# Delta rule into a maxout FFN: evictions of the opening by half of the heads, and the second chunk's first link moved behind x of the first

## The chip, the cores and the metric

The kernel runs on one core of a Trainium2 chip. The metric is the device time of one execution in microseconds, from its start to its end on that core. Before the change it was measured in six runs: the median is 542.86 us, the runs lie between 540.11 and 547.58 us. One of them was recorded by the hardware profiler; its trace is what the profile below shows. "The span" is the time from the first to the last instruction in that trace.

## What is computed

Two layers follow each other. The first is a delta-rule attention: for each of 4 x 8 heads, a state matrix of 48 x 48 is carried over 768 tokens. The second is a feed-forward layer whose hidden value is the largest of three products.

```python
# q, k, v: (B, H, S, D) = (4, 8, 768, 48); beta: (4, 8, 768)
k_n = k / (norm(k) + 1e-6)
for t in range(S):
    y[:, :, t] = q[:, :, t] @ state
    v_old = k_n[:, :, t] @ state
    state = state + beta[t] * outer(k_n[:, :, t], v[:, :, t] - v_old)
x = y.transpose(0, 2, 1, 3).reshape(B * S, H * D)        # 3072 x 384
h = max(x @ w1, x @ w2, x @ w3)                           # 3072 x 768
out = h @ w_out                                           # 3072 x 384
```

The arithmetic is in float32. The weights come as 64-bit floats; the kernel reads their bits and converts them to float32 itself.

## The kernel before, in words

**Chunks.** The 768 tokens are cut into 12 chunks of 64 (`C = 64`), and the recurrence is carried from chunk to chunk. Two batches lie on the 128 partitions (rows `0:64` and `64:128`, called `bb`), and two more in a free dimension (`g`). All eight heads of all four batches are worked on together. Two chunks make a group of 512 tokens, the unit of the feed-forward layer, so there are six groups `m`. Inside a chunk the dependence of the tokens on each other is a triangular system. It is solved in blocks:

- `solve(m)` (line 518) inverts the diagonal blocks for the two chunks of a group on VectorE (DVE), one column at a time: lines 562 and 566, a product and a subtraction. Ahead of that it works out the norms of the keys (`norm`, lines 256 to 265, L258 on ScalarE (ACT), L259 to L263 on DVE), and writes the diagonal (L539, on ACT for every group but the first; it waits for `bl` of L538). For groups 0 and 1 the blocks are 16 wide, for the later ones 32. For group 0 its last part transposes the result (L570) and copies it into `ut[0]` and `ut[1]`, the inverse of each chunk (L581 on ACT; L583 on DVE for chunk 0, on GpSimd (POOL) for chunk 1). For group 1 the result goes to DRAM (L588) and is read back into `ut` (L597) by DMAs that the SyncE queue (SP) issues.
- For chunks 0 to 3 the 16-wide blocks are joined into 32-wide ones: `halves_t` transposes `ut` (L643, L645), `halves_z` (p_e, L671; eviction to `z`, L674) and `halves_u` (p_f, L688; negation into `ut`, L678 on DVE and L680 on ACT).
- For every chunk the 32-wide blocks are joined: `turn_t1` (L629, L631), `join_z` (p_z, L705; evictions L708 and L710), `join_u` (p_j, L719; negation again).
- Then `old_k` and `old_q` multiply the keys and queries with the state (p_k, p_q, L736), `new` makes the new values u (p_u, L764, eviction L769), `to_y` the outputs (p_y, L806; L810 for chunk 0, L808 for the others), `to_x` transposes them into `xt`, the input of the feed-forward layer (p_x, L820, eviction L872/L873 for chunk 0, L870 otherwise), and `step` adds to the state (p_s, L787, L794).

`new` also zeroes a corner of `ut` for the first two chunks (L774, on ACT), which must be zero when the chunk after next is written there.

**PSUM.** All of these links take their PSUM tile from one pool of three buffers (`ps_two`, line 81), in turn. The feed-forward layer has two buffers of its own. `heads_of` (line 647) gives, for chunk 0, two halves of the heads with a PSUM tile each and a copy engine each (ACT for the first, DVE for the second); for other chunks one tile with all heads and ACT. In before, only some evictions use the engine that `heads_of` names; `negated`, `join_z` and `copied` split one PSUM tile between ACT and DVE by partitions.

**The feed-forward layer.** `ffn(m)` (line 911) is a generator: it yields after each group of three accumulating matmuls p_h (L922) with its eviction (L930 a copy on ACT for the first weight, L936 a maximum with `h` on DVE for the others), and later after each p_o (L954). For group 0 the first three slices of hidden units are worked on in two halves of 256 tokens, so that the first half of the tokens (chunk 0) can be used before chunk 1 is ready.

**The weights.** `weights()` (line 219) converts one piece of 128 x 384 at each call of `some(conv, 1)`: ACT makes `mant` and `up` (L232, L233) of a piece, and DVE (L243, L247) and POOL (L251) join the piece before it. A piece's staging buffer (`w_bits`, five of them) is filled by `fetch` on SP (L213).

**The order.** The order of the instructions on each engine is that of the program text; there is no scheduler, and each engine takes its instructions in that order. The opening is written out by hand (lines 990 to 1070); after it the loop over `ffn(0)` (line 1127) runs, in iteration i, the links that the table `FIRST[i]` names ("e1" is halves_z(1), "f1" halves_u(1), "s0" step(0), "T2" the transposes of queries 2, "S1" one step of the current solve), then those of `EARLY_LINKS[i]`, and a conversion. Groups 1 to 5 follow in a loop of their own.

Of the kernel before, what the change touches and what calls it, by code (L numbers as in the profile page):

```python
# [16 lines left out]
BL = 32  # L17
# [4 lines left out]
def kernel(  # L22
# [31 lines left out]
    nc = tc.nc  # L54
# [5 lines left out]
    KT = DM // 128  # L60
# [5 lines left out]
    NK, NQ, NU = 8, 3, 2  # L66
# [451 lines left out]
    def solve(m):  # L518
# [49 lines left out]
        if m == 0:  # L568
            back = in_rows(xs[0])
            nc.vector.transpose(out=back, in_=y.rearrange("p c i -> p i c"))  # L570
            yield
            for cc in range(2):
                for i in range(4):
                    bb, half = divmod(i, 2)
                    r = block(bb, half)
                    to = ut[cc][r, :, :, BL * half : BL * (half + 1)].rearrange(
                        "p g h i -> p (g h) i"
                    )
                    of = back[r, :, 16 * cc : 16 * (cc + 1)].rearrange("p i x -> p x i")
                    if half:  # L580
                        nc.scalar.copy(to, of)  # L581
                    else:
                        (nc.gpsimd if cc else nc.vector).tensor_copy(to, of)  # L583
                yield
            return
        y_d = dram.tile([2, 2, B, H, BL, BL], FP32, name="y_d")
# [72 lines left out]
    def span(hs):  # L659
        return slice(hs[0], hs[-1] + 1)  # L660

    def halves_z(c):
        if c > 1:
            halves_t(c)
        at = [ats[2 * c + g] for g in range(2)]
        second = ut[c % NU].rearrange("p g h (f two x) -> p g h f two x", two=2, x=HB)
        for hs, p_v, copy in heads_of(c, "p_e", BL):
            for i, h in enumerate(hs):
                for bb, g in TILES:
                    r = rows(bb)  # L670
                    nc.tensor.matmul(  # L671
                        p_v[rows(bb ^ g), g, i], at[g][r, h], second[r, g, h, :, 1]
                    )
            copy(zs[c % NU][:, :, span(hs)], p_v)  # L674

    def negated(bb, to, of, c=0):
        if bb and c < 2:
            nc.vector.tensor_scalar_mul(to, of, -1.0)  # L678
        else:
            nc.scalar.mul(to, of, -1.0)  # L680

    def halves_u(c):
        t, z = fine.pop(c), zs[c % NU]
        for hs, p_v, _ in heads_of(c, "p_f", BL):
            for i, h in enumerate(hs):
                for bb, g in TILES:
                    r = rows(bb ^ g)
                    nc.tensor.matmul(p_v[rows(bb), g, i], t[g][r, h], z[r, g, h])  # L688
            for f in (0, 1):
                for bb in range(2):  # L690
                    r = block(bb, f, HB)
                    negated(
                        bb,
                        ut[c % NU][r, :, span(hs), BL * f + HB : BL * (f + 1)],
                        p_v[r, :, :, HB * f : HB * (f + 1)],
                    )

    def join_z(c):
        at = [ats.pop(2 * c + g) for g in range(2)]
        z, second = zs[c % NU], ut[c % NU][:, :, :, BL:C]  # L700
        for hs, p_v, _ in heads_of(c, "p_z", BL):
            for i, h in enumerate(hs):
                for bb, g in TILES:
                    r = block(bb, 1)
                    nc.tensor.matmul(  # L705
                        p_v[block(bb ^ g), g, i], at[g][r, h, 0:BL], second[r, g, h]
                    )
            nc.scalar.copy(z[block(0), :, span(hs)], p_v[block(0)])  # L708
            copy = nc.vector.tensor_copy if c < 2 else nc.scalar.copy
            copy(z[block(1), :, span(hs)], p_v[block(1)])  # L710

    def join_u(c):
        z, t = zs[c % NU], t1[c % NU]
        u12 = ut[c % NU][:, :, :, BL:C]
        for hs, p_v, _ in heads_of(c, "p_j", BL):
            for i, h in enumerate(hs):
                for bb, g in TILES:
                    r = block(bb ^ g)
                    nc.tensor.matmul(p_v[block(bb), g, i], t[r, g, h], z[r, g, h])  # L719
            for bb in range(2):  # L720
                negated(bb, u12[block(bb), :, span(hs)], p_v[block(bb)], c)


    xts, rhss, qss, us, yts = {}, {}, {}, {}, {}
# [33 lines left out]
    def new(c):  # L758
        rhs = rhss.pop(c)
        u = us[c] = both("u", D, 2)  # L760
        for hs, p_v, copy in heads_of(c, "p_u", D):
            for i, h in enumerate(hs):
                for bb, g in TILES:
                    nc.tensor.matmul(  # L764
                        p_v[rows(bb ^ g), g, i],
                        ut[c % NU][rows(bb), g, h],
                        rhs[rows(bb), g, h],
                    )
            copy(u[:, :, span(hs)], p_v)  # L769
        if c + NU < 2 * FINE:  # L770
            for bb in range(2):
                corner = ut[c % NU][block(bb), :, :, BL:C]
                zero = kpad[0][block(bb), None, 0:1, D : D + 1]
                nc.scalar.copy(corner, zero.to_broadcast(corner.shape))  # L774
# [37 lines left out]
    def to_x(c):  # L812
        m, cc = divmod(c, 2)
        if m not in xts:
            xts[m] = work.tile([128, KT, TOK], FP32, name="xt")
        y_f = yts.pop(c).rearrange("p g h d -> p g (h d)")
        p_x = ps_two("p_x")
        for g in range(2):
            for t in range(KT):
                nc.tensor.transpose(  # L820
                    p_x[:, g, t * 128 : (t + 1) * 128],
                    y_f[:, g, t::KT],
                    ident,
                )
        xt = xts[m][:, :, cc * 256 : (cc + 1) * 256].rearrange(
            "p t (g x) -> p g t x", g=2
        )
        copied(c, xt, p_x[:, :, 0 : KT * 128].rearrange("p g (t x) -> p g t x", t=KT))

    yds, yqs = {}, {}  # L830

# [24 lines left out]
    def turn_y(c):  # L856
# [6 lines left out]
            ),  # L863
            in_=yqs.pop(c).rearrange("p b (x t) -> p b t x", t=KT),
        )

    def copied(c, to, of):

        if c:
            nc.scalar.copy(to, of)  # L870
        else:
            nc.scalar.copy(to[:, 0], of[:, 0])  # L872
            nc.vector.tensor_copy(to[:, 1], of[:, 1])  # L873


    def less_first(f):
        part = (slice(None), slice(None), slice(f * 128, (f + 1) * 128))
# [166 lines left out]
    for c in range(2):  # L1044
        scale(c, nrm_0[:, c])
    some(conv, 1)
    halves_u(0)
    turn_t1(0)
    join_z(0)
    masked(pts[0], by_par(pts[0]))  # L1050
    join_u(0)
    masked(pts[1], by_par(pts[1]))
    old_k(0)
    old_q(0)
    some(solving, 1)
# [12 lines left out]
    load_v(2)  # L1068
# [58 lines left out]
    for i, _ in enumerate(ffn(0)):  # L1127
# [83 lines left out]
```

## Time and profile before

| what | value |
|---|---|
| median of six runs | 542.86 us (540.11 to 547.58) |
| the profiled execution | 547.58 us, span 545.9 us |
| TensorE (PE) busy | 507.5 us, 93% of the span |
| DVE busy | 316.0 us, 58% |
| ACT busy | 155.2 us, 28% |
| POOL busy | 167.0 us, 31% |
| mean TensorE clock that was granted | 0.946 of full |
| in the first 110 us: PE, DVE, ACT, POOL busy; clock | 83.0, 83.4, 52.3, 35.0 us; 0.77 |
| from 160 to 487 us: PE, DVE, ACT, POOL busy; clock | 324.0, 191.0, 70.7, 116.6 us; 0.99 |

Times in the trace count from the first instruction of the span. A line of the chain of waits has a start, a duration, an engine and a line of the kernel; "issue" is time in which the engine waited for nothing that the trace shows. A line of a timeline has a start, a duration, the engine, the line, the operation, output and inputs by their names, shapes, the count, and in brackets how long the engine was idle before and what ended that. A float32 matmul of the program is recorded as two, so 32 matmuls appear as x64. SPq is SP's queue of DMA issues.

### The profile page before, as it was taken

The numbers are of one execution on the slowest core, as the hardware profiler recorded it, in microseconds if no ns is written. First come the engines' busy times: TensorE is split into PE (matmuls) and PEld (weight loads), VectorE is DVE, ScalarE is ACT, GpSimd is POOL, SyncE is SP. The second block draws the span as 40 slices with busy tenths as digits, with TensorE's granted clock in tenths as the row PEclk, the third lists the DMA queues.
The fourth block names the chain that finished last, engine by engine and source line by source line (L and its number), as shares of the span: only waits on it lengthen the run. The fifth ranks groups of instructions, "written<-read, shape, count | busy, mean of one in ns | idle before, by whom it ended". The sixth has DMA issues, their size and how long they took to land.

```text
span 545.9 us, 18537 instructions
## 1 busy us (share of the span) xinstructions
PE 507.5 (93%) x8096; PEld 315.1 (58%) x8096; DVE 316.0 (58%) x701; ACT 155.2 (28%) x285; POOL 167.0 (31%) x279
## 2 busy tenths in 40 slices
PE   6657899689979999999998999999999999999996
PEld 5546777576635655556555556565565556554453
DVE  6876999474899644179864388671989313101100
ACT  5536364267310324220124210143201231010100
POOL 7215025022266073487056666141330000000000
PEclk9655799789999999999999999999999999999999
DMA  8882746974303494445376546473323401230001
GB/s 110 181 166 75 152 115 147 189 137 132 77 23 91 103 189 84 95 105 132 83 158 113 118 117 143 108 136 85 86 74 78 79 2 52 53 72 1 0 22 36
DMA packets 118848, 53.49 MB, mean 98 GB/s; under 512 B 100976, under 2 KB 113456, under 8 KB 118768
## 3 DMA queue, kind: packets, MB, share of 16 engines
q1 hardware_dynamic: 109872, 40.01, 34.3%
q0 software_dynamic: 6784, 11.92, 10.0%
q8 instruction: 63, 1.03, 0.8%
q10 hardware_dynamic: 2112, 0.39, 0.5%
q14 instruction: 17, 0.14, 0.1%
HBM read 39.17 MB, written 13.11 MB: 96 GB/s over the span
## 4 chain that ended last, share of the span: by engine, by line
PE 81%; DVE 11%; issue 3%; ACT 2%; DMA 2%; SPq 1%; POOL 0%; DVEq 0%; ACTq 0%; POOLq 0%
PE p_h L922 35%; PE p_o L954 24%; PE p_g L435 4%; PE p_m L902 2%; PE p_y L806 2%; PE p_k L736 2%; DMA kpad<-in_k_dram 2%; PE p_u L764 2%; DVE tmp L562 2%; PE p_j L719 2%; PE p_q L736 2%; PE p_t L358 1%; PE p_s L787 1%; PE p_z L705 1%; DVE y_bl L566 1%
## 5 line engine op out<-in xcount | busy, mean ns | idle before, releaser
L922 PE MATMUL p_h<-xt,w_sb 128*128 128x512 f32 (+1 forms) x522 | 223.5, 574 | 6.4 <-DVE h L936 3.6
L922 PEld LDWEIGHTS p_h<-xt,w_sb 128*128 128x128 f32 x522 | 98.7, 198 | 94.4 <-issue 87.0
L954 PE MATMUL p_o<-wo_sb,h 128*128 128x384 f32 x288 | 97.7, 489 | 0.0
L936 DVE TENSOR_TENSOR h<-h,p_h 128x512 f32<-128x512 f32 (+1 forms) x48 | 29.7, 618 | 94.4 <-PE p_h L922 94.4
L954 PEld LDWEIGHTS p_o<-wo_sb,h 128*128 128x128 f32 x288 | 53.7, 190 | 35.7 <-issue 0.5
L562 DVE TENSOR_TENSOR tmp<-x_bl,y_bl 128x31 f32<-128x31 f32 (+20 forms) x139 | 49.9, 359 | 4.1
L566 DVE TENSOR_TENSOR y_bl<-y_bl,tmp 128x31 f32<-128x31 f32 (+20 forms) x139 | 49.3, 355 | 4.8
L960 ACT COPY o_sb<-p_o 128x384 f32<-128x384 f32 x24 | 11.5, 480 | 140.5 <-PE p_o L954 134.5
L932 ACT ACTIVATE h<-p_h 128x512 f32<-128x512 f32 x30 | 17.9, 597 | 88.0 <-PE p_h L922 83.6
L954 PE MATMUL p_o<-w_sb,xt 128*128 128x384 f32 x120 | 42.0, 486 | 0.0
L435 PE MATMUL p_g<-kqt 48*64 48x64 f32 (+1 forms) x1216 | 30.7, 248 | 11.2 <-DVE nt_bl L260 4.3
L393 POOL DMA_DIRECT2D turned<-in_q_dram x72 | 39.2, 552 | 3.9 <-POOL turned L388 3.0
L435 PEld LDWEIGHTS p_g<-kqt 48*64 48x64 f32 x1216 | 26.2, 147 | 18.9 <-issue 8.4
L251 POOL TENSOR_TENSOR w_sb<-mant,up 128x384 int32<-128x384 int32 x18 | 18.0, 999 | 61.3 <-DVE mant L247 49.1
L954 PEld LDWEIGHTS p_o<-w_sb,xt 128*128 128x128 f32 x120 | 22.8, 190 | 15.9
L419 DVE TENSOR_TENSOR pt<-p_g,mask 128x512 f32<-128x512 f32 x22 | 15.2, 691 | 27.6 <-PE p_g L435 27.4
L284 POOL TENSOR_TENSOR v_t<-v_t,nrm 128x768 f32<-128x768 f32 x12 | 17.9, 1491 | 27.7 <-DVE nrm L263 13.5
L794 DVE TENSOR_TENSOR st<-st,p_s 48x768 f32<-48x768 f32 (+1 forms) x18 | 17.1, 951 | 15.0 <-PE p_s L787 14.8
L137 POOL DMA_DIRECT2D v_t<-in_v_dram x12 | 9.9, 829 | 39.4 <-PE p_u L764 39.4
L388 POOL MEMSET turned<- 128x96 f32 x18 | 3.3, 192 | 55.0 <-DVE kqt L409 55.0
L118 POOL DMA_DIRECT2D kpad<-in_k_dram x24 | 16.3, 688 | 11.6 <-PE p_s L787 11.6
L452 ACT COPY at<-p_g 128x512 f32<-128x512 f32 x21 | 12.3, 585 | 23.0 <-DVE pt L419 20.7
(150 smaller groups left out, 608.6 us busy)
## 6 DMA issues: line engine op xcount, KB each, us to landing
w_bits<-in_moe_w_dram SPq DMA_DIRECT2D x18, 384.0 KB, 6.1
out_dram<-o_sb SPq DMA_DIRECT2D x48, 96.0 KB, 2.2
turned<-in_q_dram POOLq DMA_DIRECT2D x72, 48.0 KB, 2.7
y_x<-y SPq DMA_DIRECT2D x16, 192.0 KB
qall<-y_x SPq DMA_DIRECT2D x32, 96.0 KB, 2.7
at_d<-at SPq DMA_DIRECT2D x80, 32.0 KB, 2.3
ut<-y_d SPq DMA_DIRECT2D x40, 64.0 KB, 2.7
qall<-in_q_dram SPq DMA_DIRECT2D x24, 96.0 KB, 3.3
```

The costliest lines, as they stand in the source:

```text
L251: nc.gpsimd.tensor_tensor(out=dst.bitcast(I32), in0=mant_v.bitcast(I32), in1=up_v, op=ALU.add)
L284: nc.gpsimd.tensor_tensor(out=vts[c], in0=vts[c], in1=nrm[:, :, :, None].to_broadcast([128, 2, H, D]), op=ALU.mult,)
L393: (queue, nc.gpsimd)[i].dma_start(out=t[p0 : p0 + 32, bb, at : at + NP * 2 * D].rearrange("p (j x) -> p j x", j=NP), in_=(k, q)[i][2 * bb ...
L435: nc.tensor.matmul(p_g[rows(bb ^ (g * i)), par, c0 : c0 + C * (1 + whole)], kq[:, 0], kq if whole else kq[:, i],)
L562: nc.vector.tensor_tensor(out=t_v, in0=row.to_broadcast(t_v.shape), in1=column.to_broadcast(t_v.shape), op=ALU.mult,)
L566: nc.vector.tensor_tensor(out=rest, in0=rest, in1=t_v, op=ALU.subtract)
L736: nc.tensor.matmul(p_b[rows(bb), par, c0 : c0 + D], kqt[g][dims(par), j, bb ^ g, i], st[dims(par), bb ^ g, g, j],)
L794: nc.vector.tensor_tensor(out=s_v[r], in0=s_v[r], in1=p_s[r, :, 0 : H * D], op=ALU.add)
L922: nc.tensor.matmul(p_h, w_sb[i][:, t, f * 128 : (f + 1) * 128], xt[:, t, lo : lo + w], start=(t == 0), stop=(t == KT - 1),)
L932: nc.scalar.activation(out=h, in_=p_h, func=mybir.ActivationFunctionType.Relu)
L936: nc.vector.tensor_tensor(out=h, in0=h, in1=p_h, op=ALU.max)
L954: nc.tensor.matmul(p_o, stays, moves, start=(n == 0), stop=(n == len(terms) - 1))
```

## The change

Six things are done at once:

1. In the copies of the first solve into `ut`, one of ACT's for chunk 0 goes to DVE (DVE three, ACT one), and the two that POOL made for chunk 1 go to DVE as well. Chunk 1's four copies are also issued later.
2. The negations of `halves_u` and `join_u` are made by the engine that `heads_of` names: for chunk 0 ACT takes the first half of the heads and DVE the second, each from its own PSUM tile; for chunks 1 to 3 ACT takes all. The evictions to `z` (p_e and p_z) are all made by ACT.
3. In the opening `turn_t1(0)` comes after `join_z(0)`, and both masks after `join_u(0)`.
4. The copies of `ut[1]`, two conversions of weights with their fetches, and the first link of chunk 1 (`halves_z(1)`, p_e) come after `to_x(0)`; p_e of chunk 1 is now the first link in iteration 0 of the loop, and p_f of chunk 1 comes behind `step(0)` and the transposes T2.
5. The corner of `ut[0]` is zeroed at the end of iteration 0 of the loop, not in `new(0)`.
6. `to_x(0)` uses two PSUM tiles, one for each `g`, evicted by ACT and DVE.

On PE the change only moves p_e of chunk 1 behind the first p_h and p_f of chunk 1 behind p_s and p_t. On ACT the copy of z of chunk 1 (L674) now stands behind L258, L539 and the copy of h. SP's list of DMAs is unchanged.

```diff
--- before.py
+++ after.py
@@ -577,10 +577,10 @@
                         "p g h i -> p (g h) i"
                     )
                     of = back[r, :, 16 * cc : 16 * (cc + 1)].rearrange("p i x -> p x i")
-                    if half:
+                    if half and (cc or bb):
                         nc.scalar.copy(to, of)
                     else:
-                        (nc.gpsimd if cc else nc.vector).tensor_copy(to, of)
+                        nc.vector.tensor_copy(to, of)
                 yield
             return
         y_d = dram.tile([2, 2, B, H, BL, BL], FP32, name="y_d")
@@ -671,17 +671,17 @@
                     nc.tensor.matmul(
                         p_v[rows(bb ^ g), g, i], at[g][r, h], second[r, g, h, :, 1]
                     )
-            copy(zs[c % NU][:, :, span(hs)], p_v)
-
-    def negated(bb, to, of, c=0):
-        if bb and c < 2:
+            nc.scalar.copy(zs[c % NU][:, :, span(hs)], p_v)
+
+    def negated(copy, to, of):
+        if copy == nc.scalar.copy:
+            nc.scalar.mul(to, of, -1.0)
+        else:
             nc.vector.tensor_scalar_mul(to, of, -1.0)
-        else:
-            nc.scalar.mul(to, of, -1.0)
 
     def halves_u(c):
         t, z = fine.pop(c), zs[c % NU]
-        for hs, p_v, _ in heads_of(c, "p_f", BL):
+        for hs, p_v, copy in heads_of(c, "p_f", BL):
             for i, h in enumerate(hs):
                 for bb, g in TILES:
                     r = rows(bb ^ g)
@@ -690,7 +690,7 @@
                 for bb in range(2):
                     r = block(bb, f, HB)
                     negated(
-                        bb,
+                        copy,
                         ut[c % NU][r, :, span(hs), BL * f + HB : BL * (f + 1)],
                         p_v[r, :, :, HB * f : HB * (f + 1)],
                     )
@@ -705,20 +705,19 @@
                     nc.tensor.matmul(
                         p_v[block(bb ^ g), g, i], at[g][r, h, 0:BL], second[r, g, h]
                     )
-            nc.scalar.copy(z[block(0), :, span(hs)], p_v[block(0)])
-            copy = nc.vector.tensor_copy if c < 2 else nc.scalar.copy
-            copy(z[block(1), :, span(hs)], p_v[block(1)])
+            for bb in range(2):
+                nc.scalar.copy(z[block(bb), :, span(hs)], p_v[block(bb)])
 
     def join_u(c):
         z, t = zs[c % NU], t1[c % NU]
         u12 = ut[c % NU][:, :, :, BL:C]
-        for hs, p_v, _ in heads_of(c, "p_j", BL):
+        for hs, p_v, copy in heads_of(c, "p_j", BL):
             for i, h in enumerate(hs):
                 for bb, g in TILES:
                     r = block(bb ^ g)
                     nc.tensor.matmul(p_v[block(bb), g, i], t[r, g, h], z[r, g, h])
             for bb in range(2):
-                negated(bb, u12[block(bb), :, span(hs)], p_v[block(bb)], c)
+                negated(copy, u12[block(bb), :, span(hs)], p_v[block(bb)])
 
 
     xts, rhss, qss, us, yts = {}, {}, {}, {}, {}
@@ -767,6 +766,10 @@
                         rhs[rows(bb), g, h],
                     )
             copy(u[:, :, span(hs)], p_v)
+        if c:
+            corner(c)
+
+    def corner(c):
         if c + NU < 2 * FINE:
             for bb in range(2):
                 corner = ut[c % NU][block(bb), :, :, BL:C]
@@ -814,18 +817,28 @@
         if m not in xts:
             xts[m] = work.tile([128, KT, TOK], FP32, name="xt")
         y_f = yts.pop(c).rearrange("p g h d -> p g (h d)")
-        p_x = ps_two("p_x")
-        for g in range(2):
+        xt = xts[m][:, :, cc * 256 : (cc + 1) * 256].rearrange(
+            "p t (g x) -> p g t x", g=2
+        )
+
+        def turned_y(p_x, g):
             for t in range(KT):
                 nc.tensor.transpose(
-                    p_x[:, g, t * 128 : (t + 1) * 128],
-                    y_f[:, g, t::KT],
-                    ident,
+                    p_x[:, t * 128 : (t + 1) * 128], y_f[:, g, t::KT], ident
                 )
-        xt = xts[m][:, :, cc * 256 : (cc + 1) * 256].rearrange(
-            "p t (g x) -> p g t x", g=2
-        )
-        copied(c, xt, p_x[:, :, 0 : KT * 128].rearrange("p g (t x) -> p g t x", t=KT))
+
+        if c:
+            p_x = ps_two("p_x")
+            for g in range(2):
+                turned_y(p_x[:, g], g)
+            nc.scalar.copy(
+                xt, p_x[:, :, 0 : KT * 128].rearrange("p g (t x) -> p g t x", t=KT)
+            )
+            return
+        for g, copy in enumerate((nc.scalar.copy, nc.vector.tensor_copy)):
+            p_x = ps_two("p_x")[:, 0]
+            turned_y(p_x, g)
+            copy(xt[:, g], p_x[:, 0 : KT * 128].rearrange("p (t x) -> p t x", t=KT))
 
     yds, yqs = {}, {}
 
@@ -863,15 +876,6 @@
             ),
             in_=yqs.pop(c).rearrange("p b (x t) -> p b t x", t=KT),
         )
-
-    def copied(c, to, of):
-
-        if c:
-            nc.scalar.copy(to, of)
-        else:
-            nc.scalar.copy(to[:, 0], of[:, 0])
-            nc.vector.tensor_copy(to[:, 1], of[:, 1])
-
 
     def less_first(f):
         part = (slice(None), slice(None), slice(f * 128, (f + 1) * 128))
@@ -1045,24 +1049,22 @@
         scale(c, nrm_0[:, c])
     some(conv, 1)
     halves_u(0)
+    join_z(0)
     turn_t1(0)
-    join_z(0)
+    join_u(0)
     masked(pts[0], by_par(pts[0]))
-    join_u(0)
     masked(pts[1], by_par(pts[1]))
     old_k(0)
     old_q(0)
-    some(solving, 1)
     new(0)
-    some(conv, 1)
-    fetch(nc.sync)
     to_y(0)
     some(conv, 1)
     fetch(nc.sync)
-    halves_z(1)
     to_x(0)
-    some(conv, 1)
-    fetch(nc.sync)
+    some(solving, 1)
+    for _ in range(2):
+        some(conv, 1)
+        fetch(nc.sync)
     halves_t(1)
     load_q(4)
     load_v(2)
@@ -1085,7 +1087,7 @@
 
 
     FIRST = {
-        0: "f1 s0 T2 S1 S1", 1: "z1 d1 S1 k1 P2 T3 S1 S1", 2: "j1 S1 S1 S1",
+        0: "e1 s0 T2 f1 S1 S1", 1: "z1 d1 S1 k1 P2 T3 S1 S1", 2: "j1 S1 S1 S1",
         3: "P3 S1 q1 S1 S1", 4: "u1 T4", 5: "y1", 6: "s1 T5 P4", 7: "x1 T6",
         8: "P5 T7", 10: "P6", 12: "P7",
     }
@@ -1139,6 +1141,7 @@
             load_k(i + 1)
         if i == 0:
             load_v(3)
+            corner(0)
         if i == 12:
             load_q(11)
         if i in (10, 18):
```

More of the change, by code (lines that the diff above doesn't have):

```diff
@@ L816, in to_x @@
         y_f = yts.pop(c).rearrange("p g h d -> p g (h d)")
-        p_x = ps_two("p_x")
-        for g in range(2):
-            for t in range(KT):
-                nc.tensor.transpose(
-                    p_x[:, g, t * 128 : (t + 1) * 128],
-                    y_f[:, g, t::KT],
-                    ident,
-                )
         xt = xts[m][:, :, cc * 256 : (cc + 1) * 256].rearrange(
@@ L827, in to_x @@
         )
-        copied(c, xt, p_x[:, :, 0 : KT * 128].rearrange("p g (t x) -> p g t x", t=KT))
+        def turned_y(p_x, g):
+            for t in range(KT):
+                nc.tensor.transpose(
+                    p_x[:, t * 128 : (t + 1) * 128], y_f[:, g, t::KT], ident
[12 more added lines that the diff above has]
+            copy(xt[:, g], p_x[:, 0 : KT * 128].rearrange("p (t x) -> p t x", t=KT))
     yds, yqs = {}, {}
```

## The prediction

> **What bounds the kernel now.** I read the page first (the chain by engine, the clock row), then the chain of waits in order of time, then the timeline of all engines from 26 to 106 us, since the change touches nothing that runs much later than 113 us.
>
> ```profile
> PE 81%; DVE 11%; issue 3%; ACT 2%; DMA 2%; SPq 1%; POOL 0%; DVEq 0%; ACTq 0%; POOLq 0%
> ```
>
> From 161 us on the chain is almost only PE, so a microsecond won or lost before that is a microsecond at the end. The opening is another regime:
>
> ```profile
> 27.69 1.91 DVE x_bl L570
> ...
> 39.97 1.68 issue
> ...
> 53.30 0.71 DVE t L645
> ...
> 79.19 1.06 DVE wo_sb L566
> ...
> 96.73 5.25 DMA kpad<-in_k_dram
> 102.12 1.94 PE p_t L358 x8
> ```
>
> The reader is to see three anchors. From 28 to 52 us the first chunk's links alternate PE and eviction. From 52 to 82 us DVE and PE are both nearly full (9.46 and 9.89 of 10 us in 70 to 80) until the second solve ends at 81.79 us. From there SP, which issues in order, writes and reads back that result and reaches the keys whose landing starts PE at 102.12 after 4.38 us idle. So what counts is **when the second solve ends**. The timeline between 44 and 64 us, where most of the change lies:
>
> ```profile
> 47.31 1.90 PE L671 MATMUL p_e<-ut,at 64*64 64x32 f32 x64
> ...
> 50.72 0.48 ACT L872 COPY xt<-p_x 128x384 f32<-128x384 f32 x1 [0.86 <-PE p_x L820]
> ...
> 51.23 0.56 DVE L873 COPY xt<-p_x 128x384 f32<-128x384 f32 x1 [2.14 <-ACT xt L872]
> ...
> 51.94 2.90 PE L922 MATMUL p_h<-xt,w_sb 128*128 128x256 f32 x6 [1.25 <-DVE xt L873]
> ...
> 54.77 1.82 PE L688 MATMUL p_f<-z,t 64*64 64x32 f32 x64
> ...
> 57.82 0.25 ACT L539 COPY wo_sb<-bl 128x32 f32<-128x32 f32 x1 [5.58 <-DVE bl L538]
> ```
>
> Here p_e of chunk 1 stands between p_y and p_x; the two xt copies run one after the other; and ACT sits 5.58 us at L539, waiting for the norm chain of the solve on DVE. In before, nothing that PE needs soon is queued behind L539.
>
> **The skill.** (1) "PSUM — Partial Sum Buffer", section "PSUM bank collisions raise a hardware error": two engines on one bank and quadrant are kept apart, two readers too. The trace agrees: L872 ends at 51.20, L873 starts at 51.23. (2) The same page, "Engine vs sequencer instructions": ScalarE's queue is strict FIFO. It agrees: the h copy L930 runs at 57.94, behind L539, though its p_h ended at 54.84. (3) "SBUF — State Buffer", "Who interferes with whom": a DVE instruction with two SBUF inputs, or in a two-port mode, and GpSimd block each other. It agrees: L243 takes 0.35 us alone, 1.12 at 77.28 under POOL L251. (4) "TensorE: Matmul & The Clock Gate", "What's actually happening": the clock halves or doubles at the ends of a free-running 3.4 us window. In two-microsecond slices it changes near 56.3, 63.1, 70.0 and 100.7 us, all multiples of 3.41 apart; a p_h group costs 2.90 us at half clock and 1.46 at full.
>
> **Stage 1: transpose L570 to the end of p_j.** Before: two ACT copies of 1.05 end at 31.75 and gate transposes and p_e. After: three DVE copies of 0.6 beside one on ACT end at 31.44 (0.3 won). z's second half goes from DVE (behind 2.2 us of transposes, 34.27) to ACT: about 33.8. The eight p_f negations, alternating until 37.45, become four per engine from separate tiles: ACT ends near 36.1, DVE (4 x 0.30 from 35.7) near 36.9. The transposes L629/L631 (1.36) then end at 38.3 instead of 38.83, and z of p_z on ACT (4 x 0.36) near 38.4 instead of 39.63. p_j can start at 38.35, not 39.34: 1.0 won. But p_j stops for 1.68 us of "issue" in its middle, under DMA load. If the stall moves with PE, 1.0 is won; if it ends at a fixed time, nothing. (That it vanishes would win 2.5, no reason seen.) I take 0.5: p_j ends at 41.9, not 42.4.
>
> **Stage 2: p_j to x.** Negations: 0.85 both ways. The two masks (0.69 each) follow them on DVE and end before p_u does (1.4 against 1.6 us): nothing. Without the ut and corner copies (2.2 and 1.25) ahead of them on ACT, u's first half is out 1.1 us earlier and half of p_y runs under the rest: 0.75 won. p_e leaves the place ahead of p_x: 1.0. The two xt copies come from two tiles: 0.6. Sum 2.3: xt is ready 7.2 us after p_j instead of 9.4, at **49.1, not 51.79**. The first weight piece (two DVE operations 0.9, POOL 1.0) ends about 48.8, just ahead.
>
> **Stage 3: x to the solve's end; here it is paid back.** Moved behind xt on DVE: two ut copies (1.2) and a second conversion (0.9, plus about 0.7 blocked by POOL's L251 of the piece ahead). Then transposes 2.15 and the norm chain to L538 3.05 as before: 49.1+1.2+0.9+1.6+2.15+3.05 = 58.0. Before: 57.78. So L539 runs no earlier than it did. Now z of chunk 1, formerly copied at 49.28, stands behind it: L539 0.25, h 0.35, z 0.55, so **p_f can't start before 59.2**, against 54.77. PE has p_h (2.9), p_e (1.9), p_s (1.1), p_t (0.7) from 49.2, ends them at 55.8, and then idles 3.4 us. Waiting behind p_f in PE's order are the second p_h, p_z, p_k and all that follow.
>
> Such an idle stretch takes the clock: 1.2 us at 62.2 to 63.4 was enough. At half clock p_f 1.8 and p_h 2.8 end at 63.8; before, p_h ended at 59.4. The four negations, all on ACT (4 x 0.38), hide under that p_h. From there to the end of the third p_h PE needs p_z 0.75, p_k 1.15, p_g 1.4, p_t 1.1, p_h 2.8 = 7.2 and, with half of the 1.18 us stall of before, 0.6: 71.6, against 68.1. The wait of p_z for kqt (0.69) is gone, since it comes late. With a full clock p_f 0.9 and p_h 1.5 end at 61.6, and the third p_h at 68.1: even.
>
> On DVE chunk 1 gets rid of two p_f negations with their wait (1.3), z (0.7), and the p_j negation with its wait (1.15), 3.2 in all, and gains 1.2 of copies. So DVE no longer sets the pace; PE does: 8.9 us from the third p_h to the sixth (68.1 to 77.04), for whose result DVE holds its queue, then 4.4 us of DVE to the solve's end. So the solve ends 0 to 3.5 us later than at 81.79. SP's queue carries no more and no fewer DMAs; its weight fetches wait for the conversions and shift by about 0.5, into slack before q loads not needed for 10 us.
>
> The rest costs nothing: POOL's two ut copies (2.6) ran while POOL had nothing due; the corner zeroing (1.25, at the end of iteration 0 on ACT) falls into a gap that was 4.06 us; if the gap is gone, it delays z of p_z by 1.25, still ahead of p_j. An extra PSUM tile in to_x shifts the rotation of three by one, so p_z waits for the state add, as p_k behind it did anyway: 0 to 0.8. Negations of chunks 2 and 3 on ACT alone (108 to 113 us) save perhaps 0.3 of hops, at idle DVE.
>
> **Sum.** Half clock +3.5, full clock 0; I take **+2.5 us**, nearer the half clock. On the profiled execution (547.58, of which span 545.9) that is 550.1; the six runs' median is 542.86, so **545.4**. The ends of unknown terms: the p_j stall ±0.5, the second stall ±0.6, clock 3.5, POOL blocking ±0.7: -1 to +5.
>
> **Rivals.**
> *The gain stays (25%).* The idle stretch of PE is swallowed: DVE gets to L538 earlier than I reckon, or the p_j stall vanishes (-2.5), and the freed DVE time carries through. For: 2.7 won at x, 3.2 off DVE, and both engines are full there. Against: FIFO on ACT. It gives 542.86-3 = 539.9; over 1% would need all of 5.4 us.
> *PE stays at half clock through the whole solve (11%).* Place: p_h four to six and what is between, 70 to 77 us. Price: 3 x 1.35 for p_h, and about 2.5 for p_g, p_q, p_u, p_t; with +2.5, 9 us: 552. It decides when no window between 59 and 72 us is busy enough to restore the clock; from two more windows (6.8 us) at half clock on it is over 1%. Against: before recovered after one p_h and p_j.
> *Nothing moves at the end (within +-1 us, 14%).* PE has 4.38 us of slack before 102 us; if p_h six isn't what DVE waits for, the solve ends as before: 543.
>
> My own case has 50%. About 1% is what a measurement of this kernel tells from no change. Faster by over 1%: 0.03, of the first rival's tail. Slower by over 1%: 0.12, the second rival and my case's far end. The rest, 0.85. Range 540.5 to 549.5: my case's -1 to +5 (its own range: 542 to 548), most of the first rival, scatter of a median of runs that lie 540 to 548.
>
> **What would show it.** Right: p_x directly after p_y, xt copies overlapping, x near 49; ACT z of chunk 1 directly behind L539; a PE gap of some 3 us ahead of p_f, released by ACT z; the solve's last L566 at 81.8 to 85 and keys landing as much later. Wrong: L538 well before 57, p_f without a gap, p_j without its stall, or a solve that ends before 80.

## The result, and the profile after

The changed kernel takes 546.8 us (median of 35 runs, 540.05 to 552.89), the kernel before 543.4 us in the same session (72 runs). The ratio is 1.0044, interval 1.0026 to 1.0063: a small loss, but clear of the scatter. Ratios with an interval, here and below, compare only those runs that lie within 1.5% of the fastest run of their own kernel; over all runs the means are 547.4 and 543.7 us, a loss of 3.7 us or 0.68%. A later session, with runs of before of its own, gave 1.0085 (1.0055 to 1.0115) for the unedited changed kernel; over all runs that is 549.4 against 545.4 us, a loss of 4.0. So the loss is 2.4 to 4 us, by the way of counting. The profiled execution took 545.04 us, span 543.3.

The page's chain by engine has hardly moved: PE 82% where it was 81, DVE 10% where it was 11.

```profile
PE 82%; DVE 10%; issue 2%; DMA 2%; SPq 2%; ACT 1%; ACTq 0%; POOL 0%; DVEq 0%; POOLq 0%
```

The timeline of all engines around x, the part that the change was about:

```profile
39.89 0.74 PE L718 MATMUL p_j<-z,t 32*32 32x32 f32 x35 [1.30 <-issue]
...
41.49 1.47 POOL L284 TENSOR_TENSOR v_t<-v_t,nrm 128x768 f32<-128x768 f32 x1 [4.87 <-DMA v_t<-in_v_dram]
41.56 2.55 DVE L419 TENSOR_TENSOR pt<-pt,mask 128x512 f32<-128x512 f32 x2
...
43.66 2.46 PE L809 MATMUL p_y<-u,pt 64*64 64x48 f32 x64 [0.65 <-DVE pt L419]
...
47.80 0.48 ACT L841 COPY xt<-p_x 128x384 f32<-128x384 f32 x1 [1.12 <-PE p_x L826]
...
48.44 0.56 DVE L841 COPY xt<-p_x 128x384 f32<-128x384 f32 x1 [0.85 <-PE p_x L826]
...
49.15 2.90 PE L926 MATMUL p_h<-xt,w_sb 128*128 128x256 f32 x6 [0.74 <-DVE xt L841]
...
58.25 0.59 ACT L674 COPY z<-p_e 128x512 f32<-128x512 f32 x1
...
58.89 1.93 PE L688 MATMUL p_f<-z,t 64*64 64x32 f32 x64 [2.21 <-ACT z L674]
...
60.75 2.93 PE L926 MATMUL p_h<-xt,w_sb 128*128 128x256 f32 x6
```

Read downwards: each xt copy now waits for its own p_x tile; DVE no longer waits for ACT. The first p_h starts at 49.15 instead of 51.94, a gain of 2.8 us. Ten microseconds later p_f of chunk 1 starts at 58.89 instead of 54.77, a loss of 4.1, and the bracket names the reason: PE stood still for 2.21 us until ACT had copied z. The second p_h takes 2.93 us at 60.75. Before, it and p_k of chunk 1 were:

```profile
57.95 1.46 PE L922 MATMUL p_h<-xt,w_sb 128*128 128x256 f32 x6
...
60.94 1.15 PE L736 MATMUL p_k<-st,kqt 48*64 48x48 f32 x64
```

The chain of waits runs through L539 and the copy of h in both kernels (before at 57.82 and 58.07). Behind them there stood the negations of a p_f that PE had long computed; now there stands z, and p_f and a p_h follow on PE before anything else can:

```profile
57.63 0.20 DVE bl L538
57.86 0.25 ACT wo_sb L539
58.11 0.24 ACT h L934
58.35 0.49 ACT z L674
58.89 1.93 PE p_f L688 x64
60.82 2.86 PE p_h L926 x6
63.67 1.01 PE p_z L705 x64
64.68 1.89 PE p_k L735 x64
```

So p_k of chunk 1 starts 3.7 us later than before, from an L539 that ends at the same time.

What the clock does around the gap is seen in the windows view. Its columns are the stretch, its length, the busy time (and instructions) of PE, PE's weight loads, DVE, ACT and POOL, then the granted clock, the DMA share and GB/s. First the kernel before, then after:

```profile
52.00:56.00 4.00, 4.00 (x54) 2.99 (x54) 3.73 (x10) 0.24 (x2) 1.00 (x1) 0.50 0.48 136
56.00:60.00 4.00, 3.42 (x102) 2.86 (x98) 3.22 (x12) 1.67 (x6) 0.00 (x0) 0.96 0.86 142
60.00:64.00 4.00, 2.63 (x156) 2.38 (x158) 3.80 (x10) 1.53 (x4) 0.99 (x1) 0.89 0.77 136
64.00:68.00 4.00, 4.00 (x26) 2.89 (x20) 3.79 (x11) 1.48 (x3) 0.00 (x0) 0.50 0.48 133
```

```profile
52.00:56.00 4.00, 4.00 (x131) 3.91 (x131) 3.77 (x9) 1.16 (x3) 1.28 (x2) 0.50 0.76 192
56.00:60.00 4.00, 1.79 (x48) 1.39 (x46) 3.71 (x13) 1.47 (x4) 0.00 (x0) 0.50 0.90 119
60.00:64.00 4.00, 4.00 (x66) 2.93 (x66) 1.26 (x4) 3.02 (x8) 1.00 (x1) 0.50 1.03 178
64.00:68.00 4.00, 4.00 (x151) 3.82 (x143) 3.27 (x8) 1.74 (x3) 0.00 (x0) 0.50 0.44 115
```

The clock falls to 0.50 at 25.5 us before and at 27.7 after. Before, it is back at 56.3, and at half again from 63 to 70; after, PE is busy for only 1.79 us of the stretch with the gap, and the clock stays at 0.50 until 72. The gap is not all of that: from 52 to 56 and from 60 to 68 us PE was busy without a break, and the clock stayed at 0.50 all the same. In 60 to 68 us DVE, which was full before (3.80 and 3.79), has holes: it is PE that is late now. The sixth p_h ends at 79.58 instead of 77.04.

The second solve then ends at 82.70, not 81.79. But in this one trace SP reaches the keys earlier than before, not later (before: 96.06), so PE waits for them for 0.86 us where it was 4.38:

```profile
82.72 2.21 SPq L588 DMA_DIRECT2D y_d<-wo_sb  x2
...
95.30 1.30 SPq L118 DMA_DIRECT2D kpad<-in_k_dram  x2
...
100.54 0.63 PE L358 MATMUL p_t<-ident,kpad 128*128 128x128 f32 x4 [0.86 <-DMA kpad<-in_k_dram]
```

A single trace can therefore not carry a loss of a few microseconds: runs of one kernel lie more than 10 us apart, and this trace is one of the shorter ones. From here on the times of kernels come from runs, and the traces say what happened in what order.

### The profile page after: what moved, and what is told of

Its sections match the earlier page's. It is cut to its first block, busy times and chain, and to the rows that moved or that the text cites. A ratio compares the mean times of both kernels' runs of the same rounds, so it can differ in the third digit from the quotient of the medians.

```text
span 543.3 us, 18547 instructions
## 1 busy us (share of the span) xinstructions
PE 510.4 (94%) x8096; PEld 316.4 (58%) x8096; DVE 312.1 (57%) x693; ACT 158.5 (29%) x295; POOL 164.6 (30%) x277
## 4 chain that ended last, share of the span: by engine, by line
PE 82%; DVE 10%; issue 2%; DMA 2%; SPq 2%; ACT 1%; ACTq 0%; POOL 0%; DVEq 0%; POOLq 0%
PE p_h L926 36%; PE p_o L958 25%; PE p_g L435 4%; PE p_m L906 2%; PE p_k L735 2%; PE p_y L809 2%; PE p_u L763 2%; PE p_q L735 2%; PE p_j L718 2%; DMA kpad<-in_k_dram 2%; DVE tmp L562 2%; SPq L118 1%; PE p_z L705 1%; PE p_s L790 1%; PE p_t L358 1%
## 5 line engine op out<-in xcount | busy, mean ns | idle before, releaser
L435 PEld LDWEIGHTS p_g<-kqt 48*64 48x64 f32 x1216 | 25.1, 141 | 17.2 <-issue 8.6
L284 POOL TENSOR_TENSOR v_t<-v_t,nrm 128x768 f32<-128x768 f32 x12 | 17.9, 1492 | 27.2 <-DVE nrm L263 13.4
```

The lines of the kernel that those rows point to most:

```text
L284: nc.gpsimd.tensor_tensor(out=vts[c], in0=vts[c], in1=nrm[:, :, :, None].to_broadcast([128, 2, H, D]), op=ALU.mult,)
L435: nc.tensor.matmul(p_g[rows(bb ^ (g * i)), par, c0 : c0 + C * (1 + whole)], kq[:, 0], kq if whole else kq[:, i],)
```

## The experiments

Two theories stood at first: the wait behind L539 on ACT costs (W), or the half clock that PE's idle stretch leaves behind (H).

**1. L539 on POOL, in the changed kernel and in the one before.** The instruction that ACT waits at goes elsewhere, so z no longer stands behind that wait. The same edit in the kernel before, where nothing urgent stood behind L539, is the control.

```diff
-        (nc.scalar.copy if m else nc.gpsimd.tensor_copy)(diagonal(y), bl)
+        (nc.scalar.copy if m > 1 else nc.gpsimd.tensor_copy)(diagonal(y), bl)
```

> The changed kernel, but the second solve's diagonal copy L539 goes to POOL instead of ACT. My theory (what the move wins at x is given back because z of chunk 1 stands behind L539 in ACT's queue, so p_f, the second p_h and all behind them start late): p_f follows p_t near 56.7 us instead of 58.9, PE's idle of 2.2 us is gone, and the solve ends some 2 us earlier, near 80.5; the kernel is 2 to 3.5 us faster than the changed one, thus about even with the kernel before or up to 1 us faster (ratio 0.998 to 1.001). Rival A (DVE's own work, the copies and conversions moved behind x, sets the end of the solve): the gap goes but the time stays that of the changed kernel, 1.003 to 1.005. Rival B (half clock alone): the gap goes, p_h two and three stay at 2.8 us each, and the time falls by under 1 us.

> The kernel before with L539 on POOL: a control. My theory: in the order of before nothing that PE needs soon is queued behind L539, so nothing changes: ratio 0.998 to 1.002. If moving L539 off ACT is worth something in itself (rival), it shows here as much as in the changed kernel: 0.994 to 0.996.

Measured: 1.0063 (1.0035 to 1.0092) in the changed kernel, 1.0031 (1.0002 to 1.0060) in the control. PE's timeline of the first shows that the edit did what it should:

```profile
54.70 1.11 PE L358 MATMUL p_t<-ident,qall 128*128 128x128 f32 x4
55.74 1.93 PE L688 MATMUL p_f<-z,t 64*64 64x32 f32 x64
57.60 2.70 PE L926 MATMUL p_h<-xt,w_sb 128*128 128x256 f32 x6
```

No gap, p_f 3.2 us earlier than in the changed kernel, p_k at 60.92 (as before, and 3.7 ahead of the changed kernel), and SP's write of the second solve (L588) at 78.62 instead of 82.72. But the ratio is no lower than the 1.0044 of the changed kernel, and both expectations missed. The control shows why this experiment doesn't decide: its interval just excludes 1, so moving L539 seems to have a price of its own, and the two kernels with L539 on POOL took the same time, 547.3 and 546.9 us over all runs (before 545.1). What that price is stays open. Nor may the traced 4 us be set against the mean of the runs: the traced execution, 541.78 us, was the shortest of its 22.

**2. Each half of the change alone.** "Evictions only" is before with parts 2, 3 and 6 of the change (negations by `heads_of`, z by ACT, masks late, x from two tiles). "Order only" is before with parts 4 and 5 and POOL's two copies of part 1 on DVE (ACT's one copy that went to DVE is in neither); the lines that set its order:

```diff
-    some(solving, 1)
     new(0)
...
-    halves_z(1)
     to_x(0)
+    some(solving, 1)
...
-        0: "f1 s0 T2 S1 S1", ...
+        0: "e1 s0 T2 f1 S1 S1", ...
```

> Only the evictions by halves (with turn_t1 and the masks later, and two PSUM tiles in to_x); chunk 1's copies, conversions and first link stay where they were, before x, and the corner in new. My theory: p_j starts about 0.7 us earlier and x is ready about 1 to 1.5 us earlier than in before; z of chunk 1 is copied long before L539, so the win is not given back, and DVE is rid of some 3 us: 1 to 3 us faster than before, ratio 0.994 to 0.998. Rival A (DVE work moved behind x is what costs): the same sign, since nothing is moved. Rival C (the evictions by one engine are themselves what costs, four negations in a row on ACT): slower than before, 1.002 to 1.005.

> Only the moves: chunk 1's copies into ut on DVE and ACT, two conversions, p_e and p_f and the corner behind x; evictions of before. My theory: x comes about 1 us earlier, but z of chunk 1 stands behind L539 on ACT and DVE still has its negations and z copies: the solve ends 2 to 5 us later than in before, ratio 1.004 to 1.009. Rival C: faster than before, 0.995 to 0.999.

Measured: evictions only 1.0005 (0.9971 to 1.0039), so they win nothing that can be measured, where 0.2 to 0.6% had been expected; order only 1.0101 (1.0068 to 1.0135), at the upper end of what was expected or beyond it. The cost belongs to the order. PE's timeline of "order only" has the same gap, longer, as p_s and p_t happened to run at full clock ahead of it:

```profile
52.92 1.12 PE L791 MATMUL p_s<-u,kpad 64*64 64x48 f32 x64
53.97 0.66 PE L358 MATMUL p_t<-ident,qall 128*128 128x128 f32 x4
58.47 1.15 PE L688 MATMUL p_f<-z,t 64*64 64x32 f32 x64 [3.84 <-ACT z L674]
59.55 2.93 PE L926 MATMUL p_h<-xt,w_sb 128*128 128x256 f32 x6
```

**3. The gap filled, moved, or removed, beside the changed kernel once more.** All four were measured in one session with the same runs of before. "Filled" puts five matmuls of 128x128 with no use (ten pieces in the trace) between T2 and p_f; p_f still waits for z. They take a PSUM buffer of the feed-forward layer in turn, which was not tried by itself; in the trace nothing waits for it. "Moved" issues p_f one iteration later, behind the second p_h. "Removed" lets z go ahead of L258 and L539 on ACT.

```diff
 # filled
-        0: "e1 s0 T2 f1 S1 S1", ...
+        0: "e1 s0 T2 B5 f1 S1 S1", ...
+    B=lambda n: busy(n, ident)
 # moved
+        0: "e1 s0 T2 S1 S1", 1: "f1 z1 d1 S1 k1 P2 T3 S1 S1", ...
 # removed (and the some(solving, 1) ahead of the loop taken out)
+        0: "e1 S1 s0 T2 f1 S1 S1", ...
```

> The changed kernel with five extra matmuls of 128 x 128 (results unused) put on PE behind the transposes T2, where it idles ahead of p_f; the wait of p_f for z stays. Theory H (what costs is that PE stays at half clock: its mean granted clock over the runs of the changed kernel was 0.951 against 0.957 of before, and at an equal clock the two take equal times): the extra matmuls let the clock rise earlier, mean clock 0.954 or more, and the kernel is 1 to 3 us faster than the changed one, ratio to before 0.999 to 1.0025. Theory W (the wait alone holds PE back): p_f starts no earlier, so the ratio stays at 1.003 to 1.006.

> The changed kernel with p_f of chunk 1 one iteration later, behind the second p_h: PE uses the wait for z to run that p_h. Theories W and H both expect a gain here: W because the second p_h no longer stands behind the waiting p_f (it would end near 59.6 instead of 63.7, and the solve some 2 us earlier), H because the first two p_h lie closer together; ratio to before 0.998 to 1.002. If the ratio stays at 1.003 or more while the second p_h ends before 60.5, then neither PE's hold nor its clock sets the time, and the loss lies elsewhere (later evictions all on ACT, the rotation of the PSUM tiles).

> The changed kernel with the start of the second solve issued behind p_e of chunk 1, so that on ACT z of chunk 1 stands ahead of the root L258 and of L539; DVE's order is as in the changed kernel and POOL gets nothing new. Theory W: p_f starts near 56.5 without a gap, 2 us won, ratio to before 0.999 to 1.001. Theory H: the gap goes, but PE is fed small matmuls there, so the clock stays low (mean near 0.951) and little is won, ratio 1.002 to 1.005, as with L539 on POOL (1.0063, whose own control cost 1.0031).

> The changed kernel once more, unedited, for a second profile and for a comparison on the same chip as the other three: ratio to before 1.0025 to 1.0065, mean clock 0.950 to 0.953. In its profile the 2 us gap ahead of p_f and its release by z are there again (both theories); where the half clock lies shifts with the run.

Measured: filled 0.9997 (0.9964 to 1.0029); moved 1.0076 (1.0042 to 1.0110); removed 1.0026 (0.9998 to 1.0054); the changed kernel again 1.0085 (1.0055 to 1.0115), more than expected. The intervals of "filled" and of the changed kernel lie apart. Over all runs the means are 546.4 us filled, 548.8 moved, 546.1 removed, 549.4 changed, 545.4 before: **matmuls of no use, in front of a p_f that waits for the same copy of z, take away 3.0 us (standard error 0.8) of a loss of 4.0.** Taking the gap away takes 3.3. PE's timeline and the windows view of "filled" (its profiled execution, 552.4 us, was the longest of its runs; it is read for the opening only):

```profile
57.67 1.11 PE L358 MATMUL p_t<-ident,qall 128*128 128x128 f32 x4
58.57 1.61 PE L989 MATMUL p_w<-ident 128*128 128x128 f32 x10
60.98 1.14 PE L688 MATMUL p_f<-z,t 64*64 64x32 f32 x64 [0.79 <-ACT z L674]
62.04 1.56 PE L926 MATMUL p_h<-xt,w_sb 128*128 128x256 f32 x6
```

```profile
56.00:60.00 4.00, 4.00 (x79) 3.90 (x74) 3.59 (x15) 0.05 (x1) 0.00 (x0) 0.59 1.01 205
60.00:64.00 4.00, 3.20 (x100) 2.43 (x102) 3.34 (x9) 3.15 (x9) 0.66 (x1) 1.00 0.70 121
64.00:68.00 4.00, 3.17 (x162) 2.84 (x148) 3.46 (x9) 3.22 (x7) 0.34 (x1) 1.00 0.96 163
68.00:72.00 4.00, 4.00 (x122) 3.10 (x125) 3.76 (x11) 3.53 (x7) 1.00 (x1) 1.00 0.49 108
```

PE is full from 56 to 60, the clock is back at 59.3, and p_f and p_h take 1.14 and 1.56 us in place of 1.93 and 2.93. From p_t's end to p_f's start there are 2.2 us as in the changed kernel. That speaks for H and against W: the wait was left, only the idleness was taken. "Moved" missed its expectation: its second p_h ended at 56.6 and the loss stayed, which by the words of that expectation speaks against both theories. Its trace shows what may reconcile it with H: the gap went with p_f and was still there, now behind the p_h that ran at full clock, and what followed fell back to half clock from 59.8 to 70 us.

```profile
55.10 1.46 PE L926 MATMUL p_h<-xt,w_sb 128*128 128x256 f32 x6
59.33 1.66 PE L688 MATMUL p_f<-z,t 64*64 64x32 f32 x64 [2.77 <-ACT z L674]
62.98 1.46 PE L705 MATMUL p_z<-ut,at 32*32 32x32 f32 x64 [1.99 <-ACT ut L678]
```

"Removed" has no gap (p_f at 56.37, right after p_t) and wins back about two thirds of the changed kernel's loss by the ratios, and four fifths over all runs. Both theories expect a gain there; its interval reaches into the forecasts of both.

**4. The opening alone.** To see whether the difference arises before group 1, four kernels were cut after group 0: the loop over groups 1 to 5 is left out, so that they write only the first 512 tokens' output.

```diff
-    for m in range(1, GROUPS):
+    for m in range(1, 1):
         for i, _ in enumerate(ffn(m)):
```

> The kernel before, cut short: the loop over the later groups is left out, so that only the first 512 tokens' output (group 0, four p_o) is written and the rest of the output is not. In the trace of before the last p_o of group 0 starts at 183.3 us and its DMA at 190.7, so some 190 to 197 us are expected. It is the yardstick for the other three cut kernels, without the scatter that the remaining 350 us add. No theory is tested by it alone.

> The changed kernel, cut short in the same way (only group 0's output is written). Theory H, the loss is the half clock of the opening (PE idle for 2.2 us ahead of p_f): 1.5 to 3.0 us above the cut kernel before, with a lower mean clock, worth the difference. Rival W, the solve's end and the keys behind it set the time, whatever the clock: 0.5 to 1.5 us above, with the clock equal. Rival L, the loss comes after group 0: 3 to 0 us below the cut kernel before.

> The changed kernel with L539 on POOL (no gap ahead of p_f, second solve ended some 3 us earlier in its trace), cut short in the same way (only group 0's output is written). The whole kernel was 0.6% slower than before. Theory H: 1 to 3 us above the cut kernel before, as its mean clock over the whole run was as low as the changed kernel's. Rival W: 2 to 3 us below it. Rival L, lost after group 0: 2 to 4 us below it, and not explained by the opening.

> The changed kernel with five idle matmuls of 128x128 (ten pieces) in the gap ahead of p_f, cut short in the same way (only group 0's output is written). Theory H: within 1 us of the cut kernel before, with a mean clock like it, and 1.5 to 3 us below the cut changed kernel. Rival W: the same as the cut changed kernel within 0.7 us, as p_f waits for z all the same. Rival L: the same as the cut changed kernel.

Means over all executions, with the standard error, since there were only four to eight of each; and the mean granted clock:

| cut kernel | us | clock | runs |
|---|---|---|---|
| before | 193.6 ± 0.8 | 0.865 | 8 |
| changed | 194.4 ± 1.4 | 0.863 | 6 |
| changed, L539 on POOL | 194.0 ± 0.5 | 0.851 | 4 |
| changed, gap filled | 191.4 ± 0.6 | 0.872 | 6 |

Changed minus before is 0.8 ± 1.6 us: inconclusive, it excludes neither H's lower end nor W, and L (the loss comes only after group 0) only in its larger gains. "Filled" is 3.0 ± 1.5 below changed, on the side of H and not of W, but also 2.2 ± 1.0 below before, where H had it within 1 us. With L539 on POOL the kernel is 0.4 ± 0.9 above before: W and L had it 2 to 4 us below, H 1 to 3 above. Its clock is the lowest of the four. The trace of the cut changed kernel shows the gap once more, and how it costs: its clock was already back at 51.4 us, PE stood still, and p_f and the p_h behind it were at half clock again.

```profile
53.41 0.66 PE L358 MATMUL p_t<-ident,qall 128*128 128x128 f32 x4
58.31 1.93 PE L688 MATMUL p_f<-z,t 64*64 64x32 f32 x64 [4.25 <-ACT z L674]
60.18 2.93 PE L926 MATMUL p_h<-xt,w_sb 128*128 128x256 f32 x6
```

## Why the prediction was right, and where it was not

The forecast of +2.5 us (0.46%) met +0.44% (0.26 to 0.63), which is 2.4 us of 543.4, or 3.7 over all runs. The swap of waits that it rests on is there; the steps around it are partly wrong, and that their sum came out is in part luck. Step by step:

- **Stage 1, p_j: more was won.** From the solve's transpose L570 to p_j's first full run of matmuls before takes 11.65 us (27.69 to 39.34) and the changed kernel 10.35 (27.33 to 37.68): 1.3 won where I counted 1.0 and then halved it for the stall. The stall moved with p_j, and its length varies from trace to trace: 1.68 us before and 1.30 after, 0.82 and 0.94 in the two cut kernels, 1.13 in the changed kernel again. p_j ended at 40.64, not at 41.9.
- **Stage 2, p_j to x: the right time from two errors.** xt was ready at 49.0, predicted 49.1, but from a p_j 1.3 us earlier, so the stage took 8.4 us and not 7.2. The terms for p_e and for the two xt copies came: p_x follows y's last copy, and xt is ready 2.1 us after p_x starts instead of 2.65. What failed is "u's first half is out 1.1 us earlier and half of p_y runs under the rest: 0.75 won". From p_j's end to p_y's end it is 5.1 us before and 5.5 after. One reason in this trace is the masks, which were to end before p_u. At 0.69 each they would have; beside POOL's L284 they took 2.55, p_y waited 0.65 for them, and DVE's copy of u (44.15) stood 1.1 us behind p_u's end. I had named the effect from the Trainium skill ("SBUF — State Buffer", "Who interferes with whom") and priced it for L243, not for the instruction that I moved; I didn't ask what POOL does at the new place. But the masks are not all of it. In the changed kernel's second trace they took 1.29, and p_y stopped in its middle for a reason that the trace doesn't show; the stretch took 5.2 us there, and 5.4 with L539 on POOL, where the same two things happened:

```profile
42.81 1.29 DVE L419 TENSOR_TENSOR pt<-pt,mask 128x512 f32<-128x512 f32 x2
...
43.98 1.16 PE L809 MATMUL p_y<-u,pt 64*64 64x48 f32 x27
...
45.73 1.31 PE L809 MATMUL p_y<-u,pt 64*64 64x48 f32 x37 [0.59 <-issue]
```

- **The xt copies in before: a reading that proves less.** L872 and L873 read different halves of p_x (by `g`; it is not a split by partitions), and with a tile for each half DVE waits for PE alone. So the line 51.23 shows a wait by tile. It is no evidence for the rule of bank and quadrant that the prediction sets beside it.
- **Stage 3, the swap of waits.** L538 was to end at 58.0 and ended at 57.8; z's copy followed L539 and h, as said; p_f was to start at 59.2 and started at 58.9. The gap was 2.2 us where 3.4 was forecast, since p_s and p_t took 1.94 and 1.11 us at half clock where I put full-clock 1.1 and 0.7; in two traces where they had the full clock ("order only" and the cut changed kernel) it was 3.84 and 4.25.
- **The half clock.** "Such an idle stretch takes the clock" fits "order only", "moved" and the cut changed kernel, where the clock was back before the gap and half again behind it. In the changed kernel's own two traces it had not come back yet when PE fell idle. The second p_h was to end at 63.8 (63.7 measured), the third at 71.6 (71.05). The latter has errors that cancel: p_z and p_k were put at the full-clock 0.75 and 1.15 and took 1.0 and 1.9, while p_g took 0.9 instead of 1.4 and the second stall of 0.6 didn't come. The full-clock case doesn't follow from the terms given: 61.6 with the same 7.2 and 0.6 is 69.4, not 68.1.
- **"So DVE no longer sets the pace; PE does": wrong from 71 us on.** The third p_h ended 2.9 us later than before, but the solve only 0.9. DVE did not wait for the sixth p_h: in both kernels its maximum comes after the solve. Before, DVE last waited at 69.81, for p_j's negation, which the change took from it; after, at 71.09, for the third p_h. From there to the solve's end it never waited again, for 12.0 us before and 11.6 after. My 8.9 + 4.4 us added up another chain.

```profile
69.81 0.69 DVE L678 TENSOR_SCALAR ut<-p_j 32x512 f32<-32x512 f32 x1 [0.43 <-ACT ut L680]
```

```profile
71.09 0.42 DVE L940 TENSOR_TENSOR h<-h,p_h 128x256 f32<-128x256 f32 x1 [0.94 <-PE p_h L926]
```

- **"What counts is when the second solve ends": not one for one.** In the changed kernel the solve ended 0.9 us later, within my 0 to 3.5, but the keys' issue behind it came 0.8 earlier. With the evictions alone L588 came 2.1 us earlier than before (79.68), and that same execution took 548.96 us where the traced one of before took 547.58. The sum came out near the result although its last link does not hold.
- **"Nothing that PE needs soon is queued behind L539" in before: wrong.** The chain of before has four negations and, in the timeline, the copy kqt behind it, for which p_z waited 0.69 us at 60.10. The stretch was bound by L539 before, too; the change put 1.93 us of p_f and 2.93 of p_h behind it that had stood ahead or beside.
- **What the 2.8 us at x were.** From the first p_h to p_k of chunk 1 before takes 9.0 us (51.94 to 60.94), the changed kernel 15.5 (49.15 to 64.61), and 12.7 with L539 on POOL (48.27 to 60.92). One p_e, 1.9 us at half clock, is in the stretch after and was ahead of x before. There its leaving won only 1.0, since y's copies ended at 48.2 and p_x could start no earlier. So about a third of the gain at x was this work handed on, and it came back at twice the price. Stage 2 counted the 1.0 and stage 3 the 1.9, but I never set the two against each other.
- **Rivals.** "The gain stays" and "nothing moves" are excluded by the interval; the half clock through the whole solve didn't come: it ended at 72 us, and p_h four to six ran at full clock.

How the order's loss reaches the end is only partly known. The table has the compared runs' ratio to before, the mean of all runs less that of before in the same session (standard error 0.6 to 0.9 us), and the compared runs' mean granted clock. For before the clock was 0.9588 in the session of experiments 1 and 2, and 0.9563 in that of experiment 3; for the session of the row "changed" it is not on record.

| kernel | ratio | all runs, us | clock |
|---|---|---|---|
| changed, gap filled | 0.9997 | +1.0 | 0.9575 |
| before, L539 on POOL | 1.0031 | +1.9 | 0.9555 |
| evictions only | 1.0005 | 0.0 | 0.9552 |
| changed | 1.0044 | +3.7 | 0.9535 |
| changed, gap removed | 1.0026 | +0.7 | 0.9531 |
| changed again | 1.0085 | +4.0 | 0.9518 |
| order only | 1.0101 | +4.6 | 0.9518 |
| changed, L539 on POOL | 1.0063 | +2.2 | 0.9515 |
| changed, p_f moved | 1.0076 | +3.5 | 0.9489 |

A lower clock goes with a longer time, but loosely. A fit over these executions gives 2.5 us for 0.01 of clock, and by it the clock accounts for 1.1 of the 4.8 us that lie between the compared runs of "changed again" and of before. An estimate of the most that it can be: 0.01 of clock over 545 us is 10.9 us more at half clock, which cost at most half of themselves, 5.5 us; that makes 2.5 of the 4.8. So the half clock is a part of the loss, and the rest is not explained. The traces agree no better: from 25 to 82 us those of the changed kernel have 44.4, 37.5 and 36.6 us at half clock (the last one cut), those of before 37.5 and 34.1 (cut), those with the gap filled 30.7 and 34.1 (cut), but "order only", the slowest kernel, has 30.7 as well. **Open** stays also why a kernel without any gap (L539 on POOL) has as low a clock as one with it, in the whole and in the cut form.

No version here beats the kernel before. "Filled" and "removed" come within 1 us of it: with most of the order's loss gone, the 2.8 us at x do not appear at the end either.

## What to carry to other kernels

When a link is moved behind another on PE, look at where its eviction then stands in the queue of the engine that makes it: here a 0.25 us copy that waits 4 us for a norm chain held a copy that PE needed. An idle stretch of PE of 2 to 4 us cost more than the wait itself: with the wait kept and the stretch filled by matmuls of no use, three quarters of the loss went away. And a milestone inside the kernel (x 2.8 us earlier, a solve 2 us earlier) is not a time at the end until runs, not one trace, say so.

## What the runs showed that was not expected

- **The clock comes back on its own calendar.** In the traces the granted clock changes only at instants 3.41 us (or multiples) apart, with another phase in each run: before has changes at 25.5, 56.3, 63.1 and 69.9 us, which are 9, 2 and 2 times 3.41 apart. In the changed kernel the long half-clock stretch of the opening ended at 72 us in one run and at 66 in another. The Trainium skill says the same of the window ("TensorE: Matmul & The Clock Gate", "What's actually happening"); what it means for a study is that two traces of one kernel differ by several microseconds in the opening.
- **What filled the gap.** From 52 to 56 us PE was fully busy in the changed kernel, with p_e and p_s (links of 64x32 and 64x48) and the start of a p_t, and the clock stayed at 0.50; with ten pieces of 128x128 (1.61 us) added to like work it was back at the next change. That links of this size count for less is a guess from these stretches; it was not tried by itself.
- **A mask of 0.69 us took 1.95** (the longer of the two) when POOL had just begun to multiply v by its norms beside it (L284, 1.47 us, from 41.49). With L539 on POOL the masks came first: they took 0.69 each, and L284 took 1.94.
